# A transformer block on one NeuronCore: the work order handed to a list scheduler in the source, the MLP in groups of four tiles, and two of the transposes moved from TensorE to DRAM

## The chip, the cores and the metric

The kernel runs on one NeuronCore of one Trainium2 chip. The metric is the device time of one execution in microseconds. A core has five engines that run their own instruction queues in order and wait for each other by semaphores: TensorE (PE in the profile, with PEld for the loading of its stationary operand), VectorE (DVE), ScalarE (ACT), GpSimd (POOL) and SyncE (SP), which here only issues DMAs. Matmuls write to PSUM, eight banks of 128 partitions by 512 float32. DMAs move data between DRAM and SBUF on 16 DMA engines; nearly all of them are issued from SP's queue.

## The reference

One pre-norm transformer block on a sequence of 2048 positions with 512 channels, in float32:

```python
qkv  = layernorm(x) @ wqkv                       # 512 -> 3*512, 32 heads of 16
attn: position s looks at s, s-2, ..., s-14      # W = 8, dilation 2, softmax over 8
h    = x + attn_out @ wo
r    = relu(layernorm(h) @ w1 + b1) ** 2         # 512 -> 1792
out  = h + r @ w2 + b2                           # 1792 -> 512
```

## The kernel before, in words

**Precision.** Each matrix product is made of three products of float32r operands: every operand X is split into a high part (an ACT cast, `hi`, L115) and a low part (X minus the high part, `lo`, L118), and the product is high·high + low·high + high·low (`mm3`, L173). So a product of a 128x512 tile with a 512-row weight is 3 x 4 = 12 matmuls, each with 128 contracted rows.

**Tiles.** The 2048 positions are 16 tiles of 128. Positions are dealt out so that a tile's partition p holds every eighth position; the queries of one parity, four tiles, need keys and values that lie in a row of a DRAM scratch, `qkv_d`.

**Stage 1, QKV.** Each tile of x is normalised, turned by four TensorE transposes (`transposes`, L153), split, and multiplied with the weights of one of four head groups at a time, 384 columns wide (`qkv`, L427). ACT takes the product out of PSUM, and SP stores it to `qkv_d`.

**Attention** runs on DVE and POOL beside the products. An item is two queries per partition of one pair of head groups: for each half of its heads DVE multiplies query and key windows (`dots`, L270, 1024 elements per partition), sums over 16 channels, makes the softmax, and multiplies with the value windows (`weigh`, L280); POOL adds the eight products up (`add_up`, L338). There are 32 items, 64 half-items.

**Stage 2, output projection and MLP.** The items give output rows for two tiles at a time. Each output tile is turned by TensorE (`o_T`, L477), multiplied by `wo`, added to x, normalised (`h_norm`), turned again by TensorE (`h_T`, L509). The MLP takes a pair of tiles, 256 columns wide (`mlp1`, L543), for each of 14 blocks of 128 hidden channels, and adds to two accumulators (`mlp2`, L551); the last four tiles go as one group, 512 columns wide. Both parts of w1 and of w2 stay in SBUF for the whole run.

**What sets the order.** The source is written slot by slot: one block of products per slot, chores hung on slots (`at`, `after`), and a running estimate of PE and DVE time that lets attention instructions out between them (`pump`). Each engine gets its instructions in the order in which the source calls them. The two accumulators, two `mm`, two `tr`, one `qp` and one `ex` bank fill PSUM.

Of the kernel before, what the change touches and what calls it, by code (L numbers as in the profile page):

```python
# [30 lines left out]
SLOW = 1.1, 1.05
LAST = 2
LAGW = 2
DELAY = 3
WJ = 2
WARM = 18
# [3 lines left out]
def block_kernel(ctx, tc, x, wqkv, wo, w1, b1, w2, b2, out):  # L40
# [11 lines left out]


    CS = (CH + PAD) * GC
    qkv_d = dram.tile([2, G // 2, 3, 2, CH + PAD, GC], F32, name="qkv_d")

    def chain(e, g, c, r, ap):
        block = ((e * (G // 2) + g // 2) * 3 + c) * 2 + g % 2
        return bass.AP(tensor=qkv_d.tensor, offset=qkv_d.offset + block * CS + r * GC, ap=ap)

# [4 lines left out]

# [4 lines left out]
    b2_sb = const.tile([P, D], F32, name="b2_sb")  # L70
# [3 lines left out]
    wq_h = wpool.tile([P, KB, 3 * D], F32R, name="wq_h", tag="big_h")  # L74
    wq_l = wpool.tile([P, KB, 3 * D], F32R, name="wq_l", tag="big_l")
    wo_h = wpool.tile([P, KB, D], F32R, name="wo_h")
    wo_l = wpool.tile([P, KB, D], F32R, name="wo_l")
    w1_h = wpool.tile([P, KB, F], F32R, name="w1_h")
    w1_l = wpool.tile([P, KB, F], F32R, name="w1_l")
    w2_h, w2_l = {}, {}  # L80

    def row(name, shape=(P, D), dt=F32):
        return work.tile(list(shape), dt, name=name, tag="row", bufs=ROWS)

# [3 lines left out]
    due = {}  # L88
    late = {}
    now = {"slot": 0, "pe": 0.0, "dve": 0.0, "sub": 0}  # L90

    def at(delta, fn, *a):
        due.setdefault(now["slot"] + delta, []).append((fn, a))

    def after(delta, fn, *a):
        late.setdefault(now["slot"] + delta, []).append((fn, a))

    def end_slot(pe):
        now["pe"] += pe
        run(due)  # L100
        pump()
        run(late)
        now["slot"] += 1

    def run(chores):
        todo = chores.get(now["slot"], [])
        while todo:
            fn, a = todo.pop(0)
            fn(*a)

    def dve(t):
        now["dve"] += t


    def hi(dst, src):  # L115
        nc.scalar.copy(dst, src)  # L116

    def lo(eng, dst, src, h):  # L118
        eng.tensor_tensor(out=dst, in0=src, in1=h, op=ALU.subtract)  # L119

    stats = {}

    def norm_stats(key, src, delay=True):
        st = small.tile([P, 6], F32, name="st")
        mv = small.tile([P, 2], F32, name="mv", bufs=4)
        rs = small.tile([P, 2], F32, name="rs", bufs=4)
        nc.vector.bn_stats(st, src)
        nc.vector.bn_aggr(mv, st)
        dve(0.93)
        stats[key] = mv, rs  # L130

        def finish():
            nc.gpsimd.tensor_scalar(out=rs[:, 1:2], in0=mv[:, 1:2], scalar1=EPS, scalar2=None,  # L133
                                    op0=ALU.add)
            nc.gpsimd.tensor_tensor(out=rs[:, 0:1], in0=rs[:, 1:2], in1=mhalf, op=ALU.pow)  # L135
            if delay:
                nc.gpsimd.tensor_scalar(out=rs[:, 1:2], in0=mv[:, 0:1], scalar1=rs[:, 0:1],  # L137
                                        scalar2=-1.0, op0=ALU.mult, op1=ALU.mult)
        if delay:
            after(0, finish)  # L140
        else:
            finish()

    def norm_apply(key, dst, src, eng):
        mv, rs = stats.pop(key)
        if eng is nc.vector:
            nc.vector.tensor_scalar(out=dst, in0=src, scalar1=mv[:, 0:1], scalar2=rs[:, 0:1],
                                    op0=ALU.subtract, op1=ALU.mult)
            dve(0.46)
        else:  # L150
            nc.scalar.activation(dst, src, AF.Identity, scale=rs[:, 0:1], bias=rs[:, 1:2])  # L151

    def transposes(src):  # L153
        tr = psum.tile([P, KB, P], F32, name="tr", bufs=2)
        for k in range(KB):
            nc.tensor.transpose(tr[:, k, :], src[:, k * P:(k + 1) * P], ident)  # L156
        now["pe"] += 0.45
        return tr

    def parts(tr, dst):  # L160
        n = len(dst)
        return [(dst[i], tr[:, i * KB // n:(i + 1) * KB // n]) for i in range(n)]

    def hi_T(tr, h_dst):
        for d, src in parts(tr, h_dst):
            hi(d, src)

    def lo_T(tr, h_dst, l_dst):
        for (d, src), h in zip(parts(tr, l_dst), h_dst):
            lo(nc.vector, d, src, h)  # L170
            dve(0.07 + 0.54 / len(h_dst))

    def mm3(ps, lh, ll, rh, rl):  # L173

        terms = [(lh, rh, k) for k in range(KB)] + [(ll, rh, k) for k in range(KB)]
        terms += [(lh, rl, k) for k in range(KB)]
        for n, (l, r, k) in enumerate(terms):
            nc.tensor.matmul(ps, l(k), r(k), start=(n == 0), stop=(n == 3 * KB - 1))  # L178


    items = [(s, gp) for gp in range(G // 2) for s in range(RI)]
    items += [(s, gp) for s in range(RI, NS) for gp in range(G // 2)]
    stored = set()
    done = {s: 0 for s in range(NS)}
    o_t = {}

    def where(s):
        u, half = divmod(s, RI)
        b, e = divmod(u, 2)
        return u, b, e, RI * half  # L190

    def load_window(n, j, c, name):
        s, gp = items[n]
        u, b, e, i0 = where(s)
        t = att.tile([P, R + W - 1, GC], F32, name=name)
        sl = (R if u == 0 else RI) + W - 1
        nc.sync.dma_start(t[:, :sl], chain(e, 2 * gp + j, c, CH // 2 * b + 1 + i0,
                                           [[R * GC, P], [GC, sl], [1, GC]]))
        return t

    def window(t, s, *ap):

        return bass.AP(tensor=t.tensor, offset=t.offset + (RI * GC if s == 1 else 0),
                       ap=[list(t.ap[0]), [GC, RI], [GC, W], *ap])

    def load_q(n):
        s, gp = items[n]
        u, b, e, i0 = where(s)
        q = att.tile([P, 2, RI, GC], F32, name="q")
        nc.sync.dma_start(q.rearrange("p j i c -> p j (i c)"),  # L210
                          chain(e, 2 * gp, 0, PAD + CH // 2 * b + i0,
                                [[R * GC, P], [CS, 2], [1, RI * GC]]))
        return q

    def q_to_psum(q):
        qp = psum.tile([P, 2, RI, GC], F32, name="qp")
        nc.scalar.copy(qp, q)  # L217
        return qp

    def attention():  # L220

        N = len(items)

        def ready(n):
            return n < N and (items[n][0] // RI, items[n][1]) in stored

        ks, vs, qs, qps, ex = {}, {}, {}, {}, {}

        def load_k(n, j):
            if ready(n) and (n, j) not in ks:  # L230
                ks[n, j] = ks[n - 1, j] if items[n][0] == 1 else load_window(n, j, 1, "k")
                if j == 0:
                    qs[n] = load_q(n)

        def load_v(n, j):
            if ready(n) and (n, j) not in vs:
                vs[n, j] = vs[n - 1, j] if items[n][0] == 1 else load_window(n, j, 2, "v")

        while not ready(0):
            yield None  # L240
        for j in range(2):
            load_k(0, j)
        for j in range(2):
            load_v(0, j)
        for _ in range(DELAY):
            yield None
        for n in range(N + 1):

            new, old = n < N, n > 0
            while new and not ready(n):  # L250
                yield None
            if new:
                s, gp = items[n]
                u, b, e, i0 = where(s)
                for j in range(2):
                    load_k(n, j)
                if n not in qps:
                    qps[n] = q_to_psum(qs.pop(n))
                qp = qps.pop(n)
                lg = att.tile([P, RI, W, 2, GH], F32, name="lg")  # L260
                lf = lg.rearrange("p i w j h -> p i w (j h)")
                mx = small.tile([P, RI, 2 * GH], F32, name="mx")
            if old:
                s1, gp1 = items[n - 1]
                e1 = ex.pop(n - 1)
# [83 lines left out]
    def pump(until=None):  # L349

        while (done[until] < G) if until is not None else (now["dve"] < now["pe"]):
# [3 lines left out]
            for a in todo:  # L355
                add_up(*a)
# [448 lines left out]
```

## Time and profile before

| | before |
|---|---|
| time, median of 3 runs | 528.97 us (528.71 to 529.87) |
| profiled execution, span from first to last instruction | 527.5 us |
| PE busy | 518.5 us (98%), 3024 matmuls and transposes |
| DVE busy | 382.8 us (73%) |
| POOL busy | 306.6 us (58%) |
| ACT busy | 252.0 us (48%) |
| DMA | 75.93 MB, 144 GB/s over the span |
| granted TensorE clock, mean | 0.996 |

The span leaves out some 1.5 us that the timed run has around it. The profile names a group of instructions by source line, engine and operation, with tiles as out<-in, and gives the time each was busy, its mean duration, and what ended the idle time before it. Matmuls overlap in the profile, so their mean duration is longer than their spacing; spacings are read from the timeline or the chain of waits instead.

### The profile page before, as it was taken

The page shows a single profiled execution, that of the slowest core. Times are in us where ns is not written, and L with a number is a line of the kernel's source. Part 1 is how long each engine was busy: PE and PEld are TensorE (multiplying, and loading weights), DVE is VectorE, ACT ScalarE, POOL GpSimd, SP SyncE. Part 2 cuts the span into 40 slices and gives each one's busy share as a digit, 9 for nine tenths or more (in the row PEclk, how much of TensorE's full clock was granted, in tenths as well). Part 3 has the DMA queues.
Part 4 walks back from the last instruction along what each step waited for, and adds up shares of the span by engine and source line. Part 5 has one row for each costly group of instructions (what it writes and reads, how often), then busy time and mean ns, then how long its engine had stood idle before and what let it go on. Part 6 is the DMA issues. An engine that isn't in the chain of part 4 may idle for free.

```text
span 527.5 us, 8636 instructions
## 1 busy us (share of the span) xinstructions
PE 518.5 (98%) x3024; PEld 471.7 (89%) x3024; DVE 382.8 (73%) x571; ACT 252.0 (48%) x565; POOL 306.6 (58%) x421
## 2 busy tenths in 40 slices
PE   7899999999999999999999999999999999999997
PEld 6899999999999888988989898898989888888886
DVE  5559999998998799997998899699979323211113
ACT  4514554554347566545626464463536335442331
POOL 3514678788666479676877786876879717000000
PEclk8999999999999999999999999999999999999999
DMA  8578887898677453544544464454435000100002
GB/s 250 144 228 221 276 257 228 247 277 257 195 224 259 134 177 105 179 125 141 179 135 122 116 187 122 133 179 125 124 99 170 19 0 2 40 1 1 1 0 80
DMA packets 70803, 75.93 MB, mean 144 GB/s; under 512 B 6760, under 2 KB 47976, under 8 KB 70760
## 3 DMA queue, kind: packets, MB, share of 16 engines
q1 hardware_dynamic: 70616, 75.26, 47.6%
q8 instruction: 23, 0.38, 0.3%
q14 instruction: 20, 0.16, 0.1%
q10 hardware_dynamic: 144, 0.13, 0.1%
HBM read 58.50 MB, written 16.91 MB: 143 GB/s over the span
## 4 chain that ended last, share of the span: by engine, by line
PE 57%; issue 3%; POOL 3%; ACT 0%; DVE 0%; POOLq 0%; ACTq 0%
PE mm L178 25%; PE acc L560 25%; PE wo L178 5%; PE tr L156 2%; POOL rl L119 1%; POOL rs L135 1%; POOL h L497 0%; POOL pr L343 0%; PE half L581 0%; DVE pr L284 0%; POOL rs L137 0%; POOL rs L133 0%; ACT hn L151 0%; ACT r L537 0%; POOL o L343 0%
## 5 line engine op out<-in xcount | busy, mean ns | idle before, releaser
L343 POOL TENSOR_TENSOR pr<-pr 128x512 f32<-128x512 f32 (+1 forms) x128 | 131.5, 1027 | 36.8 <-DVE pr L284 31.5
L537 ACT ACTIVATE r<-mm,b_sb 128x256 f32<-128x256 f32 (+1 forms) x98 | 49.4, 505 | 120.0 <-PE mm L178 111.2
L119 POOL TENSOR_TENSOR rl<-r,rh 128x256 fp32r<-128x256 f32 x84 | 63.0, 754 | 57.6 <-ACT rh L116 57.5
L284 DVE TENSOR_TENSOR pr<-ex,v 128x1024 f32<-128x1024 f32 x64 | 78.0, 1220 | 5.5 <-POOL o L343 2.9
L273 DVE TENSOR_TENSOR pr<-qp,k 128x1024 f32<-128x1024 f32 x64 | 76.1, 1188 | 4.9 <-ACT qp L217 4.3
L178 PE MATMUL mm<-hh,w_h 128*128 128x256 f32 (+1 forms) x392 | 69.8, 300 | 0.0
L178 PE MATMUL mm<-hl,w_h 128*128 128x256 f32 (+1 forms) x392 | 69.0, 298 | 0.0
L178 PE MATMUL mm<-hh,w_l 128*128 128x256 f32 (+1 forms) x392 | 68.9, 298 | 0.0
L178 PEld LDWEIGHTS mm<-hh,w_h 128*128 128x128 f32 x392 | 59.9, 189 | 6.8 <-ACT r L537 0.2
L422 ACT COPY y<-mm 128x384 f32<-128x384 f32 x64 | 30.2, 480 | 65.3 <-PE mm L178 34.1
L560 PE MATMUL acc<-w_h,rh 128*128 128x512 f32 x192 | 58.8, 397 | 0.0
L178 PEld LDWEIGHTS mm<-hl,w_h 128*128 128x128 f32 x392 | 56.8, 191 | 2.2
L178 PEld LDWEIGHTS mm<-hh,w_l 128*128 128x128 f32 x392 | 56.7, 191 | 2.2
L560 PE MATMUL acc<-w_h,rl 128*128 128x512 f32 x192 | 57.8, 391 | 0.3 <-POOL rl L119 0.3
L560 PE MATMUL acc<-w_l,rh 128*128 128x512 f32 x192 | 57.9, 391 | 0.0
L178 PE MATMUL mm<-wq_h,xh 128*128 128x384 f32 x256 | 57.4, 344 | 0.1
L178 PE MATMUL mm<-wq_h,xl 128*128 128x384 f32 x256 | 55.6, 338 | 0.6 <-DVE xl L119 0.4
L178 PE MATMUL mm<-wq_l,xh 128*128 128x384 f32 x256 | 55.0, 335 | 0.0
L119 DVE TENSOR_TENSOR rl<-r,rh 128x512 fp32r<-128x512 f32 x14 | 9.7, 692 | 59.8 <-ACT rh L116 59.8
L178 PEld LDWEIGHTS mm<-wq_h,xl 128*128 128x128 f32 x256 | 45.9, 190 | 1.2 <-DVE xl L119 1.2
L178 PEld LDWEIGHTS mm<-wq_l,xh 128*128 128x128 f32 x256 | 45.7, 189 | 0.0
L538 ACT ACTIVATE r<-r 128x256 f32<-128x256 f32 (+1 forms) x98 | 44.0, 449 | 3.1
(84 smaller groups left out, 855.2 us busy)
## 6 DMA issues: line engine op xcount, KB each, us to landing
k<-qkv_d SPq DMA_DIRECT2D x48, 288.0 KB, 2.7
v<-qkv_d SPq DMA_DIRECT2D x48, 288.0 KB, 2.7
qkv_d<-y SPq DMA_DIRECT2D x32, 384.0 KB, 4.3
xt<-in_A_x_dram SPq DMA_DIRECT2D x16, 256.0 KB, 4.3
q<-qkv_d SPq DMA_DIRECT2D x32, 128.0 KB, 2.9
h<-in_A_x_dram SPq DMA_DIRECT2D x16, 256.0 KB, 3.8
out_dram<-h SPq DMA_DIRECT2D x15, 256.0 KB, 3.1
raw<-in_B_w_dram SPq DMA_DIRECT2D x16, 224.0 KB, 4.4
```

The costliest lines, as they stand in the source:

```text
L119: eng.tensor_tensor(out=dst, in0=src, in1=h, op=ALU.subtract)
L135: nc.gpsimd.tensor_tensor(out=rs[:, 0:1], in0=rs[:, 1:2], in1=mhalf, op=ALU.pow)
L156: nc.tensor.transpose(tr[:, k, :], src[:, k * P:(k + 1) * P], ident)
L178: nc.tensor.matmul(ps, l(k), r(k), start=(n == 0), stop=(n == 3 * KB - 1))
L273: nc.vector.tensor_tensor(out=pr.rearrange("p i w h d -> p i w (h d)"), in0=qp[:, j].unsqueeze(2).to_broadcast([P, RI, W, GC]), in1=kwin, ...
L284: nc.vector.tensor_tensor(out=p2, in1=vwin, op=ALU.mult, in0=e1[:, :, :, j * GH:(j + 1) * GH].unsqueeze(4).to_broadcast([P, RI, W, GH, DH]))
L343: nc.gpsimd.tensor_tensor(out=dst, in0=p2[:, :, :w], in1=p2[:, :, w:2 * w], op=ALU.add)
L422: nc.scalar.copy(y[:, :, t % RI * GC:(t % RI + 1) * GC], ps[:, :3 * GP].rearrange("p (j c) -> p j c", j=6))
L537: nc.scalar.activation(r, ps, AF.Relu, bias=b1_sb[:, f:f + 1])
L538: nc.scalar.activation(r, r, AF.Square)
L560: nc.tensor.matmul(acc[j], l[:, j * P:(j + 1) * P], w[f], start=(f == 0 and n < len(js)), stop=(f == last and n >= len(terms) - len(js)))
```

## The change

The source now states tasks: each has an engine (or a choice of two), a cost in microseconds, the data it reads and writes, and for some a due time. `Plan.schedule` then places them one by one: for each engine it looks for the ready task that can start first (of several, the one due first), checks that buffers are free, and books engine, buffer and a model of the DMA pipe. At the end the tasks are emitted in the order of the start times found. So the order on every engine changes everywhere. What the tasks are changes too:

- The four tiles of the first parity still run QKV by head group, 384 wide (`qkv_first`). The other twelve run q, k and v of all heads, 512 wide (`qkv`).
- An attention item is four queries of eight heads (16 items); its two halves are 2048 elements per partition. Logits and exponentials lie in one PSUM bank.
- The MLP runs in four groups of four tiles, 512 columns wide, with four accumulators. Six PSUM banks are one pool, `ps`. `w1` stays in SBUF. `w2`'s two parts are made once, written to DRAM (`w2_d`), and read back for each of the four groups, 512 KB per hidden block, through four buffers.
- Accumulators and h of the first three groups are parked in DRAM (`m_d`, `h_d`), added up and stored in the last group.
- x is still turned by TensorE. For the first group of four tiles o and h are too. For the three later groups they are turned by DRAM: `o` is written to `o_d`, h to `t_d`, read back with rows and blocks exchanged in pieces of 512 bytes, and finished by a DVE transpose of 32x32 blocks (`turn`). `to_mlp(u + 1)` is placed after block 8 of group u, `split_h` after its last `mlp1`.
- The norms of the last twelve x tiles and last twelve h tiles are made on ACT with accumulated sums.

```diff
-    def o_T(s, j):
-        pump(until=s)
-        tr = transposes(o_t[s][:, j, :])
...
-    def h_T(s, j):
...
-        tr = transposes(hn.pop((s, j)))
...
+IQ = 2
+G = 4
+FA = 6
+ITEM = 14.0
+BEFORE = 12, 16, 16, 16
+X_BY_PE = True
+LO = ("POOL",)
+BY_PE = (0,)
+TO_MLP = 8
+AHEAD = 10.0
...
+    def schedule(self):
...
+        while ready:
...
+            for eng in free:
...
+                    s = max(free[eng], ready_at[t])
+                    if t.ahead is not None:
+                        s = max(s, t.alap - t.ahead)
+                    if t.dma is not None and len(lands) >= 8:
+                        s = max(s, lands[-8])
...
+                    key = (s if s > free[eng] + 0.02 else free[eng],
+                           t.due - 1e3 if t.pe is not None and t.early else t.due, t.n)
...
+        self.order = sorted(range(len(order)), key=lambda i: (order[i].start, i))
...
+def dma_us(count, packet):
+    return count / 16 * (9 + 0.0366 * packet) / 1000
...
+    bufs = {**ROWS, "pair": 4, "unit": 1, "kv": 3, "q": 1, "pr": 3, "o": 2, "ps": 6, "qp": 1,
+            "st": 2, "mv": 4, "rs": 4, "sv": 6, "mx": 2, "sm": 2}
...
+    def turn_write(d, src):
+        load(128, 2048, lambda q: q.dma_start(
+            turn_ap(d, 0, [D, KB], [KB * D, Q], [1, D]), src.get()), r=[src], w=[("d", d)])
+
+    def turn_read(d, dst, n=1, r=(), **k):
+        load(512 * n, 512, lambda q: q.dma_start(
+            dst.get().rearrange("p (m c) -> p m c", c=P),
+            turn_ap(d, 0, [P, KB], [D, Q * n * KB], [1, P])),
+            r=list(r) + [("d", d)], w=[dst], **k)
+
+    def turn(src, dst, part=slice(None), w=()):
+        vec(D, lambda: nc.vector.transpose(dst.get(), src.get()[:, part]), r=[src],
+            w=[dst, *w])
...
+    def item(u, g, due, o):
...
+        for n, i0 in enumerate((0, IQ)):
+            pr = buf("pr", (P, IQ, W, GC), name="pr")
+            vec(2048, lambda pr=pr, i0=i0: nc.vector.tensor_tensor(
+                out=pr.get(),
+                in0=qp.get()[:, i0:i0 + IQ].unsqueeze(2).to_broadcast([P, IQ, W, GC]),
+                in1=window(ks.get(), i0, [1, GC]), op=ALU.mult),
+                r=[qp, ks], w=[pr], by=due + 5 * n)
...
+    def get_w2(f):
+        t = buf("pair", (P, 2, D), F32R, "w2s")
+        load(128, 4096, lambda q: q.dma_start(t.get().bitcast(F32), w2_d[f]), r=[("w2d", f)],
+             w=[(t, 0), (t, 1)], ahead=AHEAD)
+        return t
+
+    def mlp1(f, engs):
+        ps = buf("ps", (P, D), name="mm")
...
+        mm3(ps, ps.get, D, (lambda k: w1_of(0, f)[:, k, :], wk[0]),
+            (lambda k: w1_of(1, f)[:, k, :], wk[1]), (lambda k: big_h[:, k, :], hk[0]),
+            (lambda k: big_l[:, k, :], hk[1]), order=1)
...
+    def to_mlp(u, first):
+
+        h = {i: load_h(u * R + i) for i in range(R)}
+        if u in BY_PE:
...
+        else:
+            d = Dram(dram.tile([R * P * D], F32, name="o_d"))
+            for g in range(G):
+                o = os_[u, g]
+                load(512, 512, lambda q, g=g, o=o: q.dma_start(
+                    turn_ap(d, g * P, [D, KB], [KB * D, Q * R], [1, P]), o.get()),
+                    r=[(o, 0, g), (o, IQ, g)], w=[("d", d, g)])
+            back = buf("unit", (P, R * D), name="back")
+            turn_read(d, back, R, r=[("d", d, g) for g in range(G)], ahead=2 * AHEAD)
+            for i in range(R):
+                t = row("turned", "B")
+                turn(back, t, slice(i * D, (i + 1) * D), [("last turn",)])
+                oh, ol = split_turned(t, "o")
+                wo_product(u * R + i, (lambda k, oh=oh: oh.get()[:, k, :], [oh]),
+                           (lambda k, ol=ol: ol.get()[:, k, :], [ol]), h[i], False,
+                           first=first + 2.73 * i)
...
+    for u in range(NU):
...
+        for f in range(FB):
...
+            w2s[f] = get_w2(f)
+            hid[f] = mlp1(f, engs)
...
+            if not last and f == TO_MLP:
+                to_mlp(u + 1, need[u + 1])
+        split_h()
...
+        plan.deadlines()
+        end = plan.schedule()
+    for t in plan.order:
+        t.fn(t.on)
```

**Where the order matters, place 1: DVE ahead of the first MLP block.** `hl` and, after the change, `big_l` are the low parts of the turned h, which the MLP multiplies. Before, DVE has these rows just ahead of the first MLP product:

```order
L299 TENSOR_REDUCE lg<-pr 128x16x4
L302 RECIPROCAL sm<-sm 128x16
L273 TENSOR_TENSOR pr<-qp,k 128x1024
L308 TENSOR_TENSOR ex<-ex,sm 128x128
L284 TENSOR_TENSOR pr<-ex,v 128x1024
L313 TENSOR_REDUCE lg<-pr 128x16x4
L119 TENSOR_TENSOR hl<-tr,hh 128x2x128 x2
L318 TENSOR_TENSOR lg<-lg,mask 128x128
L284 TENSOR_TENSOR pr<-ex,v 128x1024
L119 TENSOR_TENSOR hl<-tr,hh 128x2x128 x2
```

The first MLP product there needs two tiles, and the attention items between are 1024 elements long. In the changed kernel the same place on DVE reads:

```order
L320 TENSOR_TENSOR big_l<-tr,big_h 128x4x128
L568 TENSOR_REDUCE le<-pr 128x128
L563 TENSOR_TENSOR pr<-qp,k 128x2048
L583 TENSOR_REDUCE sm<-le 128x32
L568 TENSOR_REDUCE le<-pr 128x128
L586 RECIPROCAL sm<-sm 128x32
L325 TENSOR_TENSOR le<-le,mask 128x256
L325 TENSOR_TENSOR le<-le,sm 128x256
L576 TENSOR_REDUCE mx<-le 128x32
L594 TENSOR_TENSOR pr<-le,v 128x2048 x2
L325 TENSOR_TENSOR le<-le,mx 128x256
L320 TENSOR_TENSOR big_l<-tr,big_h 128x4x128 x3
```

Four tiles are needed now, and three of the four low parts stand behind most of another attention item (its pieces read 2048 elements each, also where the row shows the smaller result).

**Place 2: from attention's output to the product with wo.** Before, on PE, inside the MLP of a pair (`mm<-hh` is mlp1, `acc` mlp2), the output is turned by a transpose:

```order
L178 MATMUL mm<-hh,w_h 128x256 x4
L178 MATMUL mm<-hh,w_l 128x256 x4
L178 MATMUL mm<-hl,w_h 128x256 x4
L156 MATMUL tr<-ident,o 128x128 x4
L178 MATMUL mm<-hh,w_h 128x256 x4
L178 MATMUL mm<-hh,w_l 128x256 x4
```

In the changed kernel it comes through SP's queue (`o_d<-o` is the write of the last head group of the second four tiles, `w2s<-w_d` the re-reading of w2, `back<-o_d` the turned read):

```order
L700 DMA w2s<-w_d 128x1024
L868 DMA o_d<-o 4x128x128
L623 DMA raw<-in_B_w_dram 128x4x128
L700 DMA w2s<-w_d 128x1024
L548 DMA v<-qkv_d 128x1408
L414 DMA back<-o_d 128x16x128
L553 DMA q<-qkv_d 128x512
L464 DMA h<-in_A_x_dram 128x512 x4
```

The transposes are gone from PE, and a write to DRAM, a 1 MB read and four DVE transposes stand in their place, with w2 and attention loads in the same queue. PE's rows around the product that waits for them are now:

```order
L449 MATMUL mm<-big_h 128x512 x4
L725 MATMUL acc<-w2s,rl 128x512 x4
L449 MATMUL wo<-wo_h,oh 128x512 x4
L449 MATMUL mm<-big_h,big_l 128x512 x4
L449 MATMUL wo<-wo_l,oh 128x512 x4
```

**Place 3: the end of a group.** Before, on PE, h of the next pair is turned among the last mlp2 blocks:

```order
L156 MATMUL tr<-ident,hn 128x128 x4
L560 MATMUL acc_2016<-w_h,rh 128x512
L560 MATMUL acc_2017<-w_h,rh 128x512
L560 MATMUL acc_2016<-w_l,rh 128x512
L560 MATMUL acc_2017<-w_l,rh 128x512
L560 MATMUL acc_2016<-w_h,rl 128x512
L560 MATMUL acc_2017<-w_h,rl 128x512
L156 MATMUL tr<-ident,hn 128x128 x4
```

In the changed kernel SP has for the second group of four tiles (`t_d<-hn` writes one normalised tile, `back<-t_d` reads it turned):

```order
L410 DMA t_d<-hn 4x32x512
L414 DMA back<-t_d 128x4x128
L700 DMA w2s<-w_d 128x1024
L410 DMA t_d<-hn 4x32x512
L868 DMA o_d<-o 4x128x128
L548 DMA k<-qkv_d 128x1408
L414 DMA back<-t_d 128x4x128
L553 DMA q<-qkv_d 128x512
L700 DMA w2s<-w_d 128x1024
L414 DMA back<-t_d 128x4x128
```

These are the last two of the four writes and the last three of the four reads; an o write of a later group and loads of w2, k and q stand between them.

More of the change, by code (lines that the diff above doesn't have):

```diff
@@ L77, in block_kernel @@
     wo_l = wpool.tile([P, KB, D], F32R, name="wo_l")
[L78 to L133, printed above, removed]
+    w1a_h = wpool.tile([P, FA, KB, P], F32R, name="w1a_h")
@@ new lines, in buf, with row, act @@
+    def buf(tag, shape, dt=F32, name=None):
+        pool = pools.get(tag, att if tag in ("kv", "q", "pr", "o") else work)
+        return Buf(tag, lambda: pool.tile(list(shape), dt, name=name or tag, tag=tag,
+                                          bufs=bufs[tag]))
+    def row(name, cls, shape=(P, D), dt=F32):
+        return buf(cls, shape, dt, name)
+    engines = {"DVE": nc.vector, "POOL": nc.gpsimd, "ACT": nc.scalar, "SP": nc.sync}
+    def act(n, fn, extra=0.0, **k):
+        return plan.add({"ACT": ac(n) + extra}, lambda e: fn(), **k)
@@ L160, in parts @@
[L160 to L178, printed above, removed]
@@ L181, in block_kernel @@
[L181 to L199, printed above, removed]
@@ new lines, in mlp2, with run, go @@
+    def mlp2(f, hid, w2s, acc, js, first, last, split_):
+        rh, rl = hid
+        def run(terms, r, lead, end):
+            def go(e):
+                for n, (l, wn, j) in enumerate(terms):
+                    nc.tensor.matmul(acc[j].get(), l.get()[:, j * P:(j + 1) * P],
+                                     w2s.get()[:, wn], start=lead and n < len(js),
+                                     stop=end and n >= len(terms) - len(js))
+            plan.add({"PE": len(terms) * 0.23}, go, r=r, w=[acc[j] for j in js])
+        one = [(rh, 0, j) for j in js] + [(rh, 1, j) for j in js]
+        two = [(rl, 0, j) for j in js]
+        if split_:
+            run(one, [rh, (w2s, 0), (w2s, 1)], first, False)
+            run(two, [rl, (w2s, 0)], False, last)
+        else:
+            one.insert(1, two[0])
+            run(one, [rh, rl, (w2s, 0), (w2s, 1)], first, last)
@@ new lines, in block_kernel @@
+    pool(0.6, consts, w=["zero_sb", "mask"], by=0.0)
+    load(192, 512, lambda q: q.dma_start(
+        chain(0, 0, 0, 0, [[GC, PAD], [CS, 6 * G], [1, GC]]),
+        zero.unsqueeze(1).to_broadcast([PAD, 6 * G, GC])), r=["zero_sb"],
+        w=["zero"] + [("S", "halo", g) for g in range(G)], by=12.0)
+    warm = buf("ps", (P, KB, P), name="tr")
+    for n in range(WARM):
+        plan.add({"PE": 0.3}, lambda e, n=n: nc.tensor.transpose(
+            warm.get()[:, n % KB, :], ident, ident), r=["ident"], w=[warm], first=-10.0)
@@ new lines, in block_kernel, with x_chain @@
+    for g in range(1, G):
+        for t in range(R):
+            qkv_first(t, g, xT[t])
+    def x_chain(t):
+        xt = load_x(t, ahead=AHEAD)
+        xn = row("xn", "A")
+        norm_act(xt, xn, "A", X_BY_PE)
+        if X_BY_PE:
+            tr = pe_turn([block(xn, k) for k in range(KB)], [xn])
+            xT[t] = split(tr, "x", ("DVE",))
+        else:
+            xT[t] = split_turned(turned(xn, "A"), "x")
+    ends = T0 + 1.8 + 16 * 2.08 + 36 * 2.73 + 3.6
+    need = [ends - 24.0 + u * (FB * 5.46 + 4 * 2.73) for u in range(NU)]
```

1154 lines of the change are left out of this document (636 added, 518 removed).

## The prediction, made before the changed kernel had run

> **What bounds the kernel now.** I read the page first: totals of the engines, then the 40 slices, then the chain that ended last.
>
> ```profile
> span 527.5 us, 8636 instructions
> PE 518.5 (98%) x3024; PEld 471.7 (89%) x3024; DVE 382.8 (73%) x571; ACT 252.0 (48%) x565; POOL 306.6 (58%) x421
> DVE  5559999998998799997998899699979323211113
> PE 57%; issue 3%; POOL 3%; ACT 0%; DVE 0%; POOLq 0%; ACTq 0%
> ```
>
> PE is busy all the time and is what the chain runs along; other engines have a few per cent of it. But DVE, at 73% over the span, is at nine tenths in most slices of the first three quarters and nearly idle in the last: it is the second bound while attention lasts. The view of busy time by stretch says the same:
>
> ```profile
> core 0: us, PE busy (x) PEld busy (x) DVE busy (x) ACT busy (x) POOL busy (x), PEclk, DMA share, GB/s
> 9.00:157.00 148.00, 145.91 (x847) 143.16 (x847) 127.03 (x189) 68.25 (x150) 93.55 (x130) 0.99 0.79 234
> 80.00:100.00 20.00, 20.00 (x121) 19.90 (x120) 19.70 (x29) 9.14 (x20) 17.64 (x24) 1.00 0.89 267
> ```
>
> A busy PE is not yet a PE at its peak, so I take its pace from the chain of waits in order of time (start, length, work) and from PE's timeline:
>
> ```profile
> 228.88 1.43 PE mm L178 x12
> 456.13 2.72 PE acc L560 x12
> 458.85 2.72 PE mm L178 x12
> ```
> ```profile
> 7.80 1.97 PE L178 MATMUL mm<-wq_h,xh 128*128 128x384 f32 x4
> 12.45 0.63 PE L156 MATMUL tr<-ident,xt 128*128 128x128 f32 x4 [0.51 <-DVE xt L147]
> 19.39 0.85 PE L178 MATMUL mm<-wq_h,xh 128*128 128x384 f32 x4
> 20.08 0.85 PE L178 MATMUL mm<-wq_h,xl 128*128 128x384 f32 x4
> 44.35 0.60 PE L156 MATMUL tr<-ident,xt 128*128 128x128 f32 x4
> 44.70 0.94 PE L178 MATMUL mm<-wq_h,xh 128*128 128x384 f32 x4
> 45.49 0.85 PE L178 MATMUL mm<-wq_h,xl 128*128 128x384 f32 x4
> ```
>
> One matmul takes 1.43/12 = 0.119 us at 256 columns, (20.08 - 19.39)/4 = 0.173 at 384, 2.72/12 = 0.227 at 512. Four transposes cost 0.35 and delay the next four matmuls by another 0.10 (0.79 instead of 0.69): 0.45. With these, the kernel's 768 matmuls of 384, 1026 of 512, 1020 of 256 and 48 sets of transposes are 133.1 + 232.6 + 121.4 + 21.6 = 508.7 us. The other 18.8 of the span are the start, a first stretch at half clock, and the end.
>
> **PE's work.** The changed kernel has 192 matmuls of 384, 1962 of 512, 12 of 256, and 24 sets of transposes: 33.3 + 444.8 + 1.4 + 10.8 = 490.3. That is 18.4 us less: 10.8 from the transposes, the rest from wider matmuls. All of it lies on the path, so it is a full gain if PE stays dense. The start keeps its 18.8: all four x tiles now go ahead of the weights, but two waits of half a microsecond fall away; I take 0, between -2 and +2.
>
> **DVE ahead of the first MLP group (place 1).** Two attention halves are now one, so fixed costs fall; but the first group needs four tiles, and DVE must have done more by then. Costs by shape:
>
> ```profile
> L284 DVE TENSOR_TENSOR pr<-ex,v 128x1024 f32<-128x1024 f32 x64 | 78.0, 1220 | 5.5 <-POOL o L343 2.9
> L273 DVE TENSOR_TENSOR pr<-qp,k 128x1024 f32<-128x1024 f32 x64 | 76.1, 1188 | 4.9 <-ACT qp L217 4.3 <-POOL o L343 0.4
> L299 DVE TENSOR_REDUCE lg<-pr 128x64 f32<-128x1024 f32 x32 | 38.7, 1208 | 0.0
> L119 DVE TENSOR_TENSOR xl<-tr,xh 128x512 fp32r<-128x512 f32 x16 | 10.9, 679 | 0.1
> L308 DVE TENSOR_TENSOR ex<-ex,sm 128x128 f32<-128x128 f32 x32 | 9.1, 285 | 0.0
> ```
>
> 512 more elements cost 1.220 - 0.679 = 0.54 us, so 2048 elements cost 2.27 to 2.30. From the first query-key product to the third of the four `big_l` DVE has 46 instructions of 2048 elements (105 us), 27 of 512 (18.4) and 49 small ones of some 0.40 (the last row and 128 elements more): 143 us, or 145 at the 98.5% that it reached from 80 to 100 us. PE has, between what releases that first product and the third MLP block, whose PSUM bank the split frees, 92 matmuls of 384, 504 of 512 and 20 sets of transposes: 139 us. So PE waits there for about 6 us. If the large pieces run at 2.2 us it is 1; if DVE only keeps the 95% or so around it, 12. After it DVE has less to do per MLP block, so this isn't paid again.
>
> **How many DMA engines a turned copy uses.** This decides the sign. Every copy leaves small end packets behind, and the page counts them:
>
> ```profile
> DMA packets 70803, 75.93 MB, mean 144 GB/s; under 512 B 6760, under 2 KB 47976, under 8 KB 70760
> k<-qkv_d SPq DMA_DIRECT2D x48, 288.0 KB, 2.7
> ...
> qkv_d<-qkv_d SPq DMA_DIRECT2D x8, 4.0 KB
> ...
> qkv_d<-zero SPq DMA_DIRECT2D x1, 96.0 KB
> b_sb<-in_B_b_dram SPq DMA_DIRECT2D x1, 7.0 KB, 4.3
> ```
>
> The list of copies (first, last and the two that matter are shown) has 286. Data pieces below 512 bytes are 384 of `zero`, 128 of the eight halo copies and 1792 of the bias, 2304 in all. With one end packet for each of 16 engines the count would be 2304 + 4576 = 6880. It is 120 less: exactly what is missing if the halo copies, whose outermost dimension is 2, ran on 2 engines (8 x 14), and `zero`, with 8 partitions, on 8. So a copy is dealt out by its outermost dimension. The new `o_d`, `t_d` and `back` copies have 4 outermost on the DRAM side and 128 partitions on the other. No copy here has two different sides; I take 4, since only 4 parts exist on both. The Trainium skill, "DMA: Bandwidth & Descriptors" (Why a DMA increments its semaphore by 16 and not by 1), states the rule for that too: as many engines as divide both sides' slowest dimension, at most 16. The packet count agrees for 2 and 8; by the rule these copies run on 4 engines.
>
> ```profile
> out_dram<-h SPq DMA_DIRECT2D x15, 256.0 KB, 3.1
> q<-qkv_d SPq DMA_DIRECT2D x32, 128.0 KB, 2.9
> 9.00:10.00 1.00, 0.93 (x4) 0.93 (x4) 0.69 (x2) 0.51 (x2) 0.00 (x0) 0.50 1.13 347
> 512.00:527.50 15.50, 12.20 (x60) 10.16 (x58) 4.91 (x8) 2.51 (x4) 0.00 (x0) 0.98 0.18 68
> ```
>
> With 512-byte pieces 16 engines moved 347 GB/s, so one engine needs 23.6 ns for a piece. The late stores (2048-byte pieces) moved 68 x 15.5 kB in 0.18 x 15.5 x 16 us of engine time: 87 ns. A 256-KB store lands after 3.1 us, 0.7 of it pieces: 2.4 fixed, and about as much for a load. So on 4 engines an `o_d` write takes 128 pieces, 3.0 + 2.4 = 5.4 us; the 1-MB `back` 512 pieces, 12.1 + 2.3 = 14.4; a `t_d` write 32 large pieces, 2.8 + 2.4; its read 3.0 + 2.3. On 16 they would take 3.2, 5.3, 3.1 and 3.1.
>
> **From the last o write to wo (place 2).** Chain: issue 0.5, write 5.4, read 14.4, DVE transpose 0.7 (no such row; by the 512-element row), ACT cast 0.6 and handovers 0.4: 22.0 us. SP issues the write only after w2 loads whose buffers PE's mlp2 has just freed; from there to the first wo product PE has 80, 72 and 64 matmuls of 512 in the three later groups: 18.1, 16.3 and 14.5 us. PE waits 3.9 + 5.7 + 7.5 = 17 us. On 16 engines the chain is 10.6 and all is hidden. Behind the wo product stand mlp1 and mlp2; on DVE the attention stands behind the transposes.
>
> **The end of a group (place 3).** From the first `t_d` write to the first mlp1 that needs all four tiles PE has 112 matmuls in the first of the three (25.4 us). The same four engines must do in that time four writes, four reads and an o write, 4 x 2.8 + 5 x 3.0, and their parts of two w2 loads, k and q, 4.0: 30.2, with 2.4 for the last landing and 1.7 for transpose and cast: 34.3. PE waits 8.9. In the next two groups PE has 140 and 120 matmuls (31.8 and 27.2) against 30.3 and 28.7: 0 and 1. So 9 in all, 0 on 16 engines, up to 20 if each read also meets a DVE instruction of 2.3 us.
>
> POOL (more `lo` work, same adds) and ACT (new norms) stay under two thirds busy; w2's loads have 14 us of PE work ahead of them; the last stores hang on nothing PE needs. These I cost at 0; a w2 load caught behind a `back` would cost what it lacks of these 14 us.
>
> **Sum.** 527.5 - 18.4 + 6 + 17 + 9 = 541.1 for the span; the runs' median is 1.5 above the profiled span: **542.6 us**, slower by 2.6%. What can be told from no change is about 0.2%, 527.9 to 530.0.
>
> **Rivals.** (a) The turned copies don't delay PE, because they run on 16 engines or the order has more slack than I count: then only PE's gain and DVE's wait are left, 527.5 - 18.4 + 6 + 1.5 = **516.6**, faster. For it: the trace has no copy with two different sides. Against: the 120 packets. (b) The clock falls in the waits. In the row of 9.00 the granted clock is 0.50, after PE had waited at the start; the 12 matmuls from 7.80 to 12.45 took 4.6 us with a 0.5 us wait in it, instead of 2.1. If each of five waits costs 2 to 2.5 more: **554**. For it: the waits I forecast are 4 to 9 us. Against: after 12 us, waits of 0.5 to 0.9 left the clock alone. The Trainium skill, "TensorE: Matmul & The Clock Gate" (Part 1), halves the clock after an idle window of about 3.4 us; by that rule all but the shortest of my waits would be followed by a slow stretch, which speaks for (b). (c) DVE doesn't hold PE up either, and nothing else does: 510.6.
>
> **How the numbers follow.** My forecast 0.45 (own range 530 to 551), (a) 0.36, (b) 0.15, (c) and the rest 0.04. The range reaches into (a) and (b): 513 to 557; below it I leave (c) and the better part of (a), above it the worse half of (b). Faster: 0.34 of (a), 0.01 of mine and 0.02 of the rest, 0.37. Same: 0.04. Slower: 0.59.
>
> **What would show it.** In the changed profile `back<-o_d` lands 14 us after issue, not 5, and `t_d` copies 5, not 3; PE's idle time before L449 `wo` and before L725 at a group's end is 17 and 9 us and ends with an ACT cast fed by DVE L420; PE's idle time before the first MLP blocks ends with DVE L320; PE needs 2.72 us per 12 matmuls elsewhere. I am wrong if the read lands in 5 us, if PE waits for w2, or if DVE or POOL fall behind in the later groups.

## The result: slower by 16%, and the profile after

| | before | after |
|---|---|---|
| time, median of 4 runs | 529.19 us (528.71 to 529.87) | 615.62 us (613.66 to 619.04) |
| ratio | | 1.164 (95% interval 1.160 to 1.168) |
| profiled span | 527.5 us | 612.9 us |
| PE busy | 518.5 us | 519.4 us |
| granted TensorE clock, mean | 0.996 | 0.925 |

The forecast was 542.6 us, the range ended at 557. The sign came out as forecast, and the places too; the size did not.

The page of the changed kernel, its totals and its chain by engine:

```profile
span 612.9 us, 6712 instructions
PE 519.4 (85%) x2280; PEld 428.2 (70%) x2280; DVE 339.7 (55%) x313; ACT 287.6 (47%) x553; POOL 315.0 (51%) x271
...
PE 51%; DMA 18%; POOL 10%; DVE 6%; issue 5%; SPq 5%; ACT 5%; POOLq 0%; DVEq 0%; ACTq 0%
```

Two things are to be seen. PE's idle time went from 527.5 - 518.5 = 9.0 us to 612.9 - 519.4 = 93.5. And PE is as long busy as before, although its work is 18.4 us less by the unit prices: 519.4 - (518.5 - 18.4) = 19.3 us of busy time that the unit prices do not hold. In the eight stretches right behind the longest waits (5 to 8.5 us each) the granted clock was 0.65 to 0.75 on average, which alone comes to 17 us: they are matmuls at half clock. So -18.4 + 84.5 + 19.3 = 85.4 us, the whole difference of the spans. DMAs now stand on the chain with 18% of the span.

Who PE waited for, longest first (engine, line, releaser: us in total, times, longest):

```profile
PE wo L449 <- ACT oh L315: 38.8, 3, 14.7
PE acc L725 <- DMA w2s<-w_d: 15.1, 2, 7.9
PE acc L725 <- ACT rh L315: 14.3, 2, 14.2
PE mm L449 <- DVE big_l L320: 10.0, 2, 8.8
PE tr L394 <- DVE xn L361: 5.4, 3, 3.0
PE mm L449 <- ACT xh L315: 2.4, 2, 2.1
```

The first row is place 2, the next two are the ends of the three groups (place 3), the fourth is place 1. The largest part of the idle time, 38.8 of 93.5 us, is the product with wo that waits for the turned o.

**Place 2.** The chain of waits ahead of the first of these products, in order of time (start, length, work):

```profile
210.19 8.20 DMA o_d<-o
218.39 0.02 issue
218.41 18.06 DMA back<-o_d
236.46 0.02 issue
236.49 0.72 DVE turned L420
237.21 0.02 issue
237.23 0.63 ACT oh L315
```

27.7 us from the write's issue to the product at 237.90. Where the 1-MB read runs alone the windows of busy time show how many DMA engines it has:

```profile
core 0: us, PE busy (x) PEld busy (x) DVE busy (x) ACT busy (x) POOL busy (x), PEclk, DMA share, GB/s
228.00:232.00 4.00, 0.00 (x0) 0.00 (x0) 0.00 (x0) 0.00 (x0) 1.23 (x2) 0.90 0.29 87
342.00:345.00 3.00, 0.00 (x0) 0.00 (x0) 0.00 (x0) 0.00 (x0) 0.00 (x0) 0.50 0.29 82
237.00:241.00 4.00, 3.10 (x7) 2.48 (x8) 4.00 (x4) 1.60 (x3) 3.07 (x3) 0.50 0.96 330
```

0.29 of 16 engines, 82 to 87 GB/s: about a quarter of what the last row shows, where the read has landed (236.46) and the loads behind it use all engines. So it is four engines; the column reads somewhat high, as it also stands over 1 where all sixteen run (1.03 in experiment 1). SP's own timeline shows what the prediction had not seen (start, length of the issue, what it issues):

```profile
218.41 0.59 SPq L414 DMA_DIRECT2D back<-o_d  x1
219.10 13.28 SPq L553 DMA_DIRECT2D q<-qkv_d  x1
...
331.82 0.55 SPq L414 DMA_DIRECT2D back<-o_d  x1
332.43 13.40 SPq L700 DMA_DIRECT2D w2s<-w_d  x1
```

An issue mostly takes 0.3 to 0.6 us. The one behind a 1-MB turned read took 13 us: it ended at 232.38, when most of the read (218.41 to 236.46) was done, and everything behind it in SP's queue stood too.

**Place 3.** ACT's timeline at the end of the first group, and PE's row that waits for it:

```profile
279.57 0.62 ACT L315 CAST big_h<-turned 128x512 fp32r<-128x512 f32 x1 [3.49 <-DVE turned L420]
291.49 0.62 ACT L315 CAST big_h<-turned 128x512 fp32r<-128x512 f32 x1 [11.31 <-DVE turned L420]
292.02 0.68 ACT L712 ACTIVATE r<-mm,b_sb 128x512 f32<-128x512 f32 x1
292.73 0.63 ACT L714 ACTIVATE r<-r 128x512 f32<-128x512 f32 x1
293.44 0.62 ACT L315 CAST rh<-r 128x512 fp32r<-128x512 f32 x1
```
```profile
294.11 3.78 PE L725 MATMUL acc<-w2s,rh 128*128 128x512 f32 x8 [14.16 <-ACT rh L315]
```

ACT waits 11.3 us for a turned tile, and the last hidden block of the group that is ending stands behind that cast. In the same row PE's 8 matmuls take some 3.6 us instead of 1.8: half clock.

### The profile page after: what moved, and what is told of

Read it like the earlier page. It is cut to its first block, busy times and chain, and to the rows that moved or that the text cites. A ratio compares the mean times of both kernels' runs of the same rounds, so it can differ in the third digit from the quotient of the medians.

```text
span 612.9 us, 6712 instructions
## 1 busy us (share of the span) xinstructions
PE 519.4 (85%) x2280; PEld 428.2 (70%) x2280; DVE 339.7 (55%) x313; ACT 287.6 (47%) x553; POOL 315.0 (51%) x271
## 4 chain that ended last, share of the span: by engine, by line
PE 51%; DMA 18%; POOL 10%; DVE 6%; issue 5%; SPq 5%; ACT 5%; POOLq 0%; DVEq 0%; ACTq 0%
PE mm L449 27%; PE acc L725 15%; PE wo L449 8%; DMA back<-o_d 6%; POOL pr L610 6%; DMA back<-t_d 3%; DMA o_d<-o 2%; SPq L700 2%; SPq L414 2%; DVE le L568 2%; DVE pr L594 1%; DMA qkv_d<-y 1%; POOL rl L320 1%; DVE pr L563 1%; DMA xt<-in_A_x_dram 1%
## 5 line engine op out<-in xcount | busy, mean ns | idle before, releaser
L725 PE MATMUL acc<-w2s,rh 128*128 128x512 f32 x444 | 116.3, 403 | 29.4 <-DMA w2s<-w_d 15.1
L610 POOL TENSOR_TENSOR pr<-pr 128x1024 f32<-128x1024 f32 (+1 forms) x64 | 117.7, 1859 | 32.1 <-DVE pr L594 32.1
L320 POOL TENSOR_TENSOR rl<-r,rh 128x512 fp32r<-128x512 f32 x56 | 73.0, 1307 | 116.0 <-ACT rh L315 110.0
L725 PEld LDWEIGHTS acc<-w2s,rh 128*128 128x128 f32 x444 | 86.1, 195 | 49.3 <-issue 16.2
L563 DVE TENSOR_TENSOR pr<-qp,k 128x2048 f32<-128x2048 f32 x32 | 72.9, 2282 | 28.8 <-POOL o L610 20.4
L568 DVE TENSOR_REDUCE le<-pr 128x128 f32<-128x2048 f32 x32 | 73.0, 2281 | 4.0 <-ACT le L581 3.4
L594 DVE TENSOR_TENSOR pr<-le,v 128x2048 f32<-128x2048 f32 x32 | 72.0, 2279 | 2.7 <-POOL o L610 2.3
L725 PE MATMUL acc<-w2s,rl 128*128 128x512 f32 x222 | 60.8, 391 | 1.3 <-POOL rl L320 1.3
L449 PE MATMUL mm<-big_h,xh 128*128 128x512 f32 (+1 forms) x208 | 53.0, 390 | 2.4 <-ACT xh L315 2.4
L449 PE MATMUL wo<-wo_h,oh 128*128 128x512 f32 x64 | 20.7, 453 | 39.4 <-ACT oh L315 38.8
L449 PE MATMUL mm<-big_h,xl 128*128 128x512 f32 (+1 forms) x208 | 50.2, 374 | 0.3 <-DVE xl L320 0.3
L725 PEld LDWEIGHTS acc<-w2s,rl 128*128 128x128 f32 x222 | 41.6, 188 | 11.7 <-POOL rl L320 3.1
```

The costliest lines, as they stand in the source:

```text
L320: lambda e: engines[e].tensor_tensor(out=dst(), in0=src(), in1=h(), op=ALU.subtract), r=r, w=w, **k)
L449: nc.tensor.matmul(ps(), l(), rr(), start=start and i == 0, stop=stop and i == len(terms) - 1)
L563: vec(2048, lambda pr=pr, i0=i0: nc.vector.tensor_tensor(out=pr.get(), in0=qp.get()[:, i0:i0 + IQ].unsqueeze(2).to_broadcast([P, IQ, W, GC ...
L568: vec(2048, lambda pr=pr, i0=i0: nc.vector.tensor_reduce(out=lg()[:, i0:i0 + IQ].rearrange("p i w h -> p (i w h)"), in_=pr.get().rearrange ...
L594: last = vec(2048, lambda p2=p2, i0=i0: nc.vector.tensor_tensor(out=p2.get(), in1=window(vs.get(), i0, [DH, GH], [1, DH]), op=ALU.mult, in ...
L610: nc.gpsimd.tensor_tensor(out=dst, in0=a, in1=b_, op=ALU.add)
```

## The experiments

All times are medians, with the kernel before at 529.2 to 529.6 us beside them.

**1. Sixteen DMA engines, same order.** Each turned copy in four parts, 32 partitions each. (Shown for the read; the writes alike.)

```diff
-        load(512 * n, 512, lambda q: q.dma_start(
-            dst.get().rearrange("p (m c) -> p m c", c=P),
-            turn_ap(d, 0, [P, KB], [D, Q * n * KB], [1, P])),
...
+        def go(q):
+            for a in range(KB):
+                q.dma_start(dst.get()[a * Q:(a + 1) * Q].rearrange("p (m c) -> p m c", c=P),
+                            turn_ap(d, a * P, [D * n * KB, Q], [D, n * KB], [1, P]))
+        load(512 * n, 512, go, r=list(r) + [("d", d)], w=[dst], **k)
```

> Each turned copy (o_d write, back read, t_d write, t_d read) is issued as four copies of 32 partitions, so that 32 or 128 is outermost on both sides; the order of every engine stays as it was. Theory A (four DMA engines per turned copy, and the queue behind them, make the waits): the first 1-MB read lands about 5 us after its issue, not 18, issues behind it no longer take 13 us, PE's waits before wo fall from 38.7 us to under 8 and those at the group ends from 29 to under 8, the half-clock stretches go with them: 533 to 548 us, most likely 540. Rival B (the new order is too tight in any case: POOL, DVE or SP's own waits end last): the copies get faster, but under 25 us of PE's waits go: over 590 us. Rival C (pieces of 512 bytes cost the same on any number of engines): the read still lands after 14 us or more, 605 to 620 us.

Measured: **546.39 us** (544.11 to 546.55), ratio 1.032 (1.031 to 1.034). Who PE waited for:

```profile
PE mm L453 <- DVE big_l L320: 9.3, 2, 8.8
PE acc L729 <- ACT rh L315: 7.1, 2, 7.0
...
PE wo L453 <- ACT oh L315: 2.0, 3, 1.3
```

and a window in which the first 1-MB read runs:

```profile
218.00:222.00 4.00, 4.00 (x19) 3.31 (x18) 3.96 (x3) 2.22 (x4) 3.96 (x3) 1.00 1.03 295
```

The waits before wo went from 38.8 to 2.0 us, the group ends from 29.4 to 7.0, the DMA share from 0.29 to 1.03. 69 us of the 86 hung on how the copies were cut. Theory A holds; B and C fall. This run alone cannot tell the number of engines from the smaller copies; experiment 3 does.

**2. The same for o alone.** h's copies stay as they were.

> Only o's way through DRAM (o_d write, 1-MB read) is issued in four copies of 32 partitions; h's copies stay on four engines. Theory A: the three waits before wo (38.7 us) and their half-clock stretches (about 7) go, the group ends (29 us) stay: 565 to 578 us. If the issue queue, stuck behind the 1-MB read, also makes the group ends late, lower than 560. Rival B (the wait only moves to the group end): over 590 us.

Measured: **575.92 us** (573.43 to 577.75). PE's waits before wo fell to 4.7 us; the group ends kept 28.8:

```profile
PE acc L730 <- ACT rh L315: 15.3, 2, 15.1
PE acc L730 <- DMA w2s<-w_d: 13.5, 3, 8.0
PE mm L454 <- DVE big_l L320: 10.9, 3, 8.8
...
PE wo L454 <- ACT oh L315: 4.7, 2, 4.2
```

o's way costs 40 us, and h's copies are the 30 that are left to experiment 1; h's copies alone were not run, so whether the two are independent is not shown in full. But the group ends kept their wait while the 1-MB read ran on sixteen engines: they do not owe it to that read.

**3. A control: four parts on four engines.** Experiment 1 also made the copies smaller. Here the o_d writes and both reads are cut in four along another dimension, so that 4 stays outermost; the t_d writes stay whole. (Shown for the read.)

```diff
...
+        def go(q):
+            for a in range(KB):
+                q.dma_start(dst.get().rearrange("p (r a c) -> p a r c", a=KB, c=P)[:, a],
+                            turn_ap(d, a * D, [P, KB], [KB * D, Q * n], [1, P]))
+        load(512 * n, 512, go, r=list(r) + [("d", d)], w=[dst], **k)
```

> A control for the run with sixteen engines, which also made the copies four times smaller: the o_d writes and both turned reads are again issued in four parts each, with the same pieces and the same order of every engine, but cut so that 4 stays the outermost dimension on the DRAM side (t_d's writes stay whole). If the number of DMA engines is what counts: 610 to 625 us, the back read still takes 16 us and more to land, and DMA is 0.25 to 0.3 busy while it runs alone. If smaller copies or more of them were the help: 540 to 565.

Measured: **602.57 us** (601.02 to 603.01), 7 us below what was expected of the engine theory and far above what the size theory expected. PE's waits, and a window and SP's row while the first read runs:

```profile
PE wo L450 <- ACT oh L315: 25.7, 3, 9.3
PE acc L726 <- DMA w2s<-w_d: 15.5, 2, 8.1
PE acc L726 <- ACT rh L315: 13.5, 2, 13.3
```
```profile
225.00:228.00 3.00, 3.00 (x14) 2.46 (x14) 2.97 (x3) 1.14 (x3) 3.00 (x3) 1.00 0.32 92
```
```profile
219.12 9.96 SPq L416 DMA_DIRECT2D back<-o_d  x4
```

So smaller parts are worth 13 us (all of it before wo), the other 12 engines 56; in these 56 is also the cut of the t_d writes, which only experiment 1 has. Why parts help at all was not followed up; the write's way to the read's issue shortened from 8.2 to 6.8 us (212.29 to 219.12) and the read from 18.1 to some 16.8.

**4. What the half clock costs.** Useless matmuls (40, 58 and 56) just ahead of the three wo products, so that PE does not stand idle; nothing else changes.

```diff
+            for i in range(idle):
+                nc.tensor.matmul(ps(), wo_h[:, 0, :P], wo_h[:, 0, :], start=True, stop=True)
```

> The changed kernel with 40, 58 and 56 useless matmuls of 512 columns (9.1, 13.2 and 12.7 us) put on PE just ahead of the three wo products that wait 10.0, 14.7 and 14.0 us; nothing else moves. They write a bank that the product then overwrites. If the clock falls because PE is idle (the rival of the prediction that priced it at 2 to 2.5 us a wait), the products after them start at 0.23 us a matmul instead of 0.45 and the time falls by 5 to 7 us, to 608 to 611. If the half clock has another cause, the time stays at 615 to 617, or rises where the useless work runs over.

Measured: **609.93 us** (608.53 to 613.21): 154 matmuls more, and 5.7 us less. The gain is net: the wait at the first group's end is 17.4 us here, where the changed kernel has 14.2. PE's timeline at the first of the three:

```profile
230.18 9.23 PE L449 MATMUL wo<-wo_h 128*128 128x512 f32 x40
239.40 1.20 PE L451 MATMUL wo<-wo_h,oh 128*128 128x512 f32 x4
240.44 1.07 PE L451 MATMUL mm<-big_h,big_l 128*128 128x512 f32 x4
```

The product follows at 0.26 us a matmul, where the changed kernel has 0.47. The granted clock from 237 to 241 us is 1.00, in the changed kernel 0.50. The half clock is a price of the wait, some 1.9 us net for each of these three.

**5. DVE's low parts first (place 1).** The four `big_l` of the first group directly behind their casts in DVE's order.

```diff
+    for t in forward:
+        plan.order.remove(t)
+        plan.order.insert(1 + max(plan.order.index(p) for p in t.preds), t)
```

> The changed kernel with DVE's four big_l of the first MLP group moved to directly behind the ACT casts that they subtract, ahead of the attention pieces; no other engine's order changes. By the prediction's term (DVE's order ahead of the first MLP block) PE's wait of 8.8 us there falls to under 3. If nothing else is late, the time falls by 7 to 9 us, to 606 to 609. Rival: the o write of the next group hangs on attention, which is now 3 us later on DVE while PE is 9 us earlier, so that the wait before the next wo grows by what was gained: 613 to 617.

Measured: **613.67 us** (613.10 to 617.55), the rival. But the gain was not lost where the rival had it. The wait for `big_l` went, and 8 us later in the trace (186.53 instead of 178.36) another of the same length begins, on PE and, ahead of it, on ACT:

```profile
195.57 2.93 PE L727 MATMUL acc<-w2s,rh 128*128 128x512 f32 x6 [9.04 <-ACT rh L315]
```
```profile
188.26 0.37 ACT L581 ACTIVATE le<-le 128x256 f32<-128x256 f32 x1 [8.49 <-DVE le L325]
```

ACT's exponential of an attention item stands ahead of the first hidden block, and waits for DVE's last step on the logits of that item (the maximum taken off). Behind it ACT still has two casts of w1, which wait 1.5 and 1.4 us for their loads. In both orders of DVE that were run, the MLP starts behind this item.

**6. The group ends mended in the order alone.** ACT's last hidden block ahead of the third cast; two w2 loads ahead of the turned reads in SP's queue.

```diff
+    for t in hidden[13]:
+        ahead(t, sorted(highs, key=lambda t: t.start)[6])
+    for n in (4, 8):
+        late = [t for t in first if t.start > reads[n + 3].start]
+        ahead(late[0], reads[n + 1])
+        ahead(late[1], reads[n + 2])
```

> The changed kernel (copies on four engines) with three places of its order mended and nothing else: at the end of the first group ACT's three instructions on the last hidden block stand ahead of the third big_h cast instead of behind it; at the end of the second and third groups two w2 loads stand in SP's queue ahead of the turned h reads instead of behind them. Theory Q (at the group ends PE waits for work that is only queued behind the turned copies): the waits of 14.2, 7.2 and 7.9 us fall to under 10 in sum, with their half-clock stretches: 588 to 598 us. Theory T (the turned copies themselves are too slow, as the prediction had it): PE runs on for the 3 to 6 us of freed work and then waits for big_h at the next group's first mlp1; the sum stays over 20 us: 605 to 616.

Measured: **620.35 us** (617.01 to 624.71), above theory T's own bound of 616. The waits moved to the products that need the turned h, as the prediction had placed them:

```profile
PE wo L451 <- ACT oh L316: 35.6, 3, 12.7
PE mm L451 <- ACT big_h L316: 30.5, 4, 11.5
```

The copies themselves are too slow; what stood behind them in a queue had only taken the wait upon itself.

**7. Sixteen engines with fewer issues.** t_d written in one copy by 128 rows and read in four; o_d laid out so that the 1-MB read is one copy of 8-KB pieces; four issues priced at 2.3 us of SP. (`whole` is o's read, `put` o's write.)

```diff
-            turn_ap(d, 0, [D, KB], [KB * D, Q], [1, D]), src.get()), r=[src], w=[("d", d)])
+            turn_ap(d, 0, [D, P], [1, D]), src.get()), r=[src], w=[("d", d)])
...
+        def whole(q):
+            q.dma_start(dst.get(), turn_ap(d, 0, [R * D, P], [1, R * D]))
...
+                def put(q, g=g, o=o):
+                    for a in range(KB):
+                        q.dma_start(turn_ap(d, g * Q * R * D + a * P, [R * D, Q], [D, R], [1, P]),
+                                    o.get()[a * Q:(a + 1) * Q])
```

> Sixteen engines on every turned copy with fewer issues: t_d is written in one copy by 128 rows and read in four of 32 partitions; o_d is laid out so that each partition's 8 KB stand together, written in four copies and read in one. The scheduler is told that four issues take 2.3 us of SP. If what was left in the run with four copies each (546 us) was its 117 additional issues, 532 to 538; if it is DVE's and ACT's order around the first MLP group (8.8 us there) and the first group's end (7 us), 538 to 545.

Measured: **534.42 us** (533.54 to 537.94), the first of the two expectations: 12 us less than experiment 1, and the wait of 7 us at the first group's end is gone. Whether the fewer issues did this or the order that the scheduler made from the new price was not told apart. What is left is place 1, still 8.8 us.

**8. and 9. The same copies, other numbers for the scheduler.** They were chosen by the scheduler's own estimate of PE's waits. Shown for the first; the second has `TO_MLP = 10` and leaves `AHEAD` at 10.0.

```diff
-ITEM = 14.0
-BEFORE = 12, 16, 16, 16
+ITEM = 18.0
+BEFORE = 12, 22, 12, 16
...
-W2_EACH = 5.0
+W2_EACH = 8.0
...
-TO_MLP = 8
+TO_MLP = 9
...
-AHEAD = 10.0
+AHEAD = 7.0
...
-    ends = T0 + 1.8 + 16 * 2.08 + 36 * 2.73 + 3.6
+    ends = T0 + 1.8 + 16 * 2.08 + 36 * 2.73 + 14.0
...
-        w2_job(f, 85.0 + W2_EACH * f)
+        w2_job(f, 50.0 + W2_EACH * f)
```

> The same copies as in the run before, and other numbers for the scheduler, chosen by its own estimate (first MLP group due 10 us later, an item every 18 us instead of 14, BEFORE 12, 22, 12, 16, TO_MLP 9, w2 split from 50 us every 8 us, loads 7 us ahead). By its estimate PE then waits nowhere over 2.2 us (515.6 us, against 519.6 for the changed kernel, which took 615.6). With sixteen engines the estimate was 20 us low; with 5 to 10 us of that gone, 520 to 528 us: faster than the kernel before. If w2 loads 7 us ahead are too late, over 535.

> As the run before with TO_MLP 10 and loads 10 us ahead (estimate 516.0). 520 to 528 us; if the group ends, now closer to the wo products, are too short for the turned h, waits of 5 us and more there and 530 or over.

Measured: **525.87 us** (522.73 to 529.10; ratio 0.993, 0.991 to 0.995) and **520.89 us** (520.16 to 521.41; ratio 0.984, 0.981 to 0.986). The second is 1.6% below the kernel before, clear of the spread, and 15% below the changed kernel. Its engines and its longest wait (the next is 2.0 us):

```profile
PE 502.7 (97%) x2280; PEld 418.6 (81%) x2280; DVE 332.8 (64%) x312; ACT 287.3 (55%) x553; POOL 316.9 (61%) x272
```
```profile
PE tr L394 <- DVE xn L361: 5.7, 3, 3.3
```

Place 1 is gone: the first MLP group is due 10 us later and the items lie further apart. PE is busy 15.8 us less than before, near the 18.4 of the unit prices.

**10. The new order on four engines.** The numbers of experiment 9 with the changed kernel's own copies.

> The fastest order so far (TO_MLP 10, loads 10 us ahead, first MLP group later, items 18 us apart), with the changed kernel's own copies on four engines. If the order were what the changed kernel lacked: under 545 us. If the four engines make the waits whatever the order: the waits at wo and at the group ends stay at 50 us and more in sum and the time between 580 and 620; TO_MLP 10 leaves less time before the group's end than 8 did.

Measured: **619.03 us** (616.87 to 620.72). Who PE waited for:

```profile
PE acc L725 <- ACT rh L315: 33.8, 5, 16.8
PE wo L449 <- ACT oh L315: 23.7, 2, 11.9
PE wo L449 <- ACT r L712: 12.9, 1, 12.9
```

Place 2 (the last two rows) is 36.6 us, place 3 (the first row and a wait of 11.4 us for `big_h`) 45. The order alone brings nothing while the copies run on four engines; place 1 is gone here as well, and its time comes back in longer waits behind.

## Why the prediction was right in sign and wrong in size

- **PE's work, -18.4: right.** The fastest kernel has the same matmuls, and PE is busy 15.8 us less, with some stretches at half clock still in it.
- **Four DMA engines: right, shown.** 0.29 of 16 engines in the windows, 1.03 when cut otherwise, and 69 us less; the control leaves 56 of these to the engines. The step from the profile page's count of end packets agrees with these runs. So does the rule of the Trainium skill, "DMA: Bandwidth & Descriptors" (Why a DMA increments its semaphore by 16 and not by 1), that stood behind it.
- **Place 2, +17: measured 38.8.** The step that failed is the chain of 22.0 us. It took 27.7, 26.6 and 27.9 (210.19 to 237.90, 324.89 to 351.51, 434.89 to 462.78). I priced the write at 5.4 us and the read at 14.4, as if alone and at 23.6 ns a piece; the writes took 7 to 8.2, the reads 18.1 to 19.5. They were not alone: from 219 to 224 us, in the first read, DMAs moved 177 GB/s on 0.50 of 16 engines. And the price of a piece held for the first read only: alone it moved 87 GB/s, which is 23.5 ns for 512 bytes on each of four engines, the third read 68 GB/s from 448 to 456 us, 30 ns. Why the third was slower stays open. Together this is 16 us over the three groups. The other 5 are PE's cover: 17.7, 11.9 and 13.9 us of work instead of 18.1, 16.3 and 14.5; in the second group the last o write was issued 4 us behind its w2 load.
- **Place 3, +9 (8.9, 0, 1): measured 29.3 (14.2, 7.2, 7.9).** The failed step is the sum of pieces on four engines, 34.3 us in the first group, which took the engines to be always fed. In experiment 6, where PE does wait at that mlp1, it is 40.1, 39.1 and 36.5 us from the issue of the first t_d write to it (259.79 to 299.93, 370.57 to 409.65, 496.62 to 533.15), where the sum had 34.3, 30.3 and 28.7. SP's queue stood in between: two issues behind turned copies took 5.4 us each in the changed kernel (269.81, 276.81), so the copies went one after another. The place in PE's order was off too: the working has PE stop at mlp1 (its list of signs says L725, which is mlp2); it stopped at mlp2, behind ACT's and SP's queues.
- **The clock, priced at 0 in the forecast: 19.3 us in all,** 17 of them right behind eight waits. It was rival (b) with 11 us for five waits. The price of a wait was right (2 to 2.5 forecast; 1.9 on average over three in experiment 4), the number and length of waits not. By the Trainium skill, "TensorE: Matmul & The Clock Gate" (Part 1), the clock halves after about 3.4 us of idling; the row of 228 to 232 us agrees: a mean of 0.90 means 0.8 us at half clock, from 231.2 on, 3.3 us after PE's last matmul (227.88).
- **Place 1, +6: measured 8.8, and 1 at the next group.** The size came out near, in part by luck, since the reason is half right. DVE was not full, as I had it: it stood idle for POOL's adds and ACT's exponential (1.4, 1.4 and 2.4 us from 149 to 176 us), and moving its order gave nothing (experiment 5). The chain of attention items through DVE, POOL and ACT is what the first MLP group waits behind; due later, it costs nothing (experiment 9).
- **The start, 0: about 2** (waits of 6.7 us instead of 4.9 in PE's timeline of the first 20 us; after 30 us PE is 12 matmuls of 384 columns, 2.1 us, behind the kernel before). A later x tile costs a wait of 2.1 us more.
- **Rival (a), 516.6 on 16 engines:** with the changed kernel's order it is 546.4, with fewer issues 534.4, with an order made for it 520.9. For this kernel the rival was wrong, its copies ran on four engines. That copies on sixteen let nearly all of places 2 and 3 go is right; place 1, the issues and the order stood in the way of the rest.

Why so far off: each wait was a difference of two numbers of 15 to 30 us, with the smaller one nearly as large. 5 to 9 us more on each chain, which the rows of single copies in the kernel before could not show, made the waits two and three times as long.

## What to carry to other kernels

Before moving a transpose to DRAM, see what stands outermost on each side of the copy; cut it so that all engines get a share (here 32 or 128 rows outermost), and then look for the fewest issues that keep this. A wait that is predicted as a small rest of two long chains should get a range as wide as the error of the longer one, and, by these traces, every wait over 2 to 3 us a price for the half clock behind it. An order written by a scheduler is as good as its prices: here it counted on 16 engines and forecast 519.6 us for a kernel that took 615.6.

## What the runs showed of the hardware that was not expected

- A copy on few DMA engines stops the queue that issues it: one issue of SP took 13.28, 13.40 and 11.89 us behind the three 1-MB copies on four engines, where 0.3 to 0.6 is usual. Behind the same copy on sixteen (experiment 1) q's issue took 3.51 us.
- Useless matmuls in a wait made this kernel faster: 5.7 us for 154 of them.
- A shorter wait than expected halves the clock. In the changed kernel PE waited 2.1 us at 102.4 us, after 1 us of transposes, and had half the clock behind it, as the row of busy time from 105 to 108 us shows:

```profile
105.00:108.00 3.00, 3.00 (x8) 2.35 (x8) 2.97 (x5) 1.07 (x3) 3.00 (x4) 0.50 1.08 372
```

In experiment 7 a wait of 2.6 us (for h, at 397.1, without transposes) was followed by such a stretch too. In neither had the clock fallen when PE went on: it was 1.00 from 102.4 to 104.4 and 0.91 from 104.4 to 105.0, so that it fell at about 104.9, 0.4 us into the work; in experiment 7 it was 0.74 from 399.7 to 402.7, so that it fell at about 401.1, 1.4 us into it. These waits are shorter than the 3.4 us of the page of the Trainium skill named above, and the measurement decides; whether transposes count as work for the clock stays open.
